# A list-scheduled fused kernel: durations of the schedule reset, last tokens of y written by ACT and DVE into a ring of 11 slots, weight sums and weight splits given places

## The chip, the cores and the metric

The kernel runs on one core of one Trainium2 chip. The metric is the device time of one execution in microseconds (us). Differences under about 0.5% (4.9 us here) can't be told from no change.

## What is computed

Three blocks follow each other, for 8 batches of 576 tokens and a model width of 512. All arithmetic is float32; the kernel splits each operand into a high and a low part (names ending in h and l) and adds three matrix products.

```python
# attention without a score matrix: softmax of q over features, of k over tokens
x = softmax(q) @ (softmax(k, axis=tokens).T @ v)
# gated block: w_in 512x1024, token mixing w_sg 576x576, w_out 512x512
u, v = split(gelu_tanh(x @ w_in), 2)
v_n = layernorm(v) * g_ln
x = x + (u * (w_sg @ v_n + b_sg)) @ w_out
# gated convolution: w_in2 512x1024, 3 taps along tokens, w_out2 1024x512
h = relu(x @ w_in2)
y = h * sigmoid(conv3(h, conv_w))
out = y @ w_out2
```

## The kernel before

**Two stages.** The first stage (about 0 to 570 us of the span) does attention and the gated block for batches 0 to 7 and writes x to DRAM. Its loop `for b in range(B)` calls 29 groups per batch (hv, hu, pair, mx and wo in the program), and `insert` puts pieces of the attention of later batches between them. The second stage, the convolution block (from about 570 us), works feature block by feature block: 8 blocks `fc` of 128 features per batch. For one block, TensorE (PE) makes `h` (from x and w_in2, 4 steps of 128 features, for two halves of the tokens), ACT applies relu, DVE and ACT convolve into `cv`, ACT takes the sigmoid, DVE multiplies with h, and `gate` (L1219) splits y = `cv` into `yh` (ACT) and `yl` (DVE). PE then multiplies yh and yl with w_out2 (`o2`, L1247), four token tiles of 128 into the four banks `acc`. The 64 tokens that are left of 576 are collected for two batches in `yLh` and `yLl`, which have 8 blocks of 128 columns, one half for each batch, and `o2_pair` (L1261) multiplies them once per pair of batches.

**Batches 0 and 1** of the second stage run straight (`h2`, L1202). Batches 2 to 7 use a scheme with 7 products in place of 8 (`quad`, L1404), which needs sums of w_in2's quarters (`weight_sums`, L1310: 11 additions on POOL for each of two halves c, tiles `tk`, results `tn0` to `tn2`) and sums of quarters of x (`operands`, L1340). x arrives as two DRAM tensors: `load_x` loads the high part into `xf`, `add_low` (L1295) loads the low part into an `xg` tile of 3 buffers and lets POOL add it.

**POOL's copies.** `gate` lets POOL copy the last 64 columns of each yh and yl into yLh and yLl (L1228). A list `later` holds copies back while `o2` of an earlier odd batch is open, since yLh has one set of slots.

**Weight splits.** w_in2 and w_out2 are cut into 32 jobs of 256 columns (`split_far`, L1043; `split`, L460). A job has a load, 3 ACT, 4 DVE and 3 POOL operations on tiles `wsl` and `farh`, and two stores. All 32 jobs are entered at the start of batch 1 of the first stage.

**What sets the order.** No engine runs in the order in which the code is written. The code records nodes in a `Plan`; `price` (L205) gives each node a cost and a latency, `deadlines` (L243) counts back from the PE's sequence the time `late` by which each must be issued, and `order` (L259) simulates the engines and lets each take the ready node with the least `late`. The order that comes out is fixed before the run; on the chip every engine issues its list in order and waits at its head. All recorded instructions have the line of `emit`, L403, in the profile, so they are told apart by tile names.

Of the kernel before, what the change touches and what calls it, by code (L numbers as in the profile page):

```python
# [25 lines left out]
CFG = {'dord': 'qqkqqkqwkkwwv', 'start': 'kaaatabbktbkbqkTawtqbqtQvwwvxxqxswxlwLc', 'gh': 'aaa', 'x2': 'nnn', 'hvl': [6, 5, 3], 'qs': 'ppppd', 'qm': 'pppdp', 'vb': 2, 'gb': 2, 'kt': 'dddd', 'sgl': 'dppp', 'rh': 'pd', 'sw': 'ada', 'sl': 'ada', 'gl': 'ddd'}  # L26
GUARD = 1.125 * 2.0 ** -15
# [105 lines left out]
class Node:  # L133
    __slots__ = ("eng", "name", "args", "kw", "cost", "lat", "deps", "succ", "late", "unit", "shared", "table", "kb", "i", "left", "ready", "done", "t", "hook")
# [10 lines left out]
class Plan:  # L145
# [59 lines left out]
    def price(self, n, out, ins):  # L205
# [18 lines left out]
        elif e == "act":  # L224
            n.cost = 0.15 + cols * 0.00091
            n.lat = n.cost + 0.12
            f = args_func(n)
            n.table = {"Gelu_apprx_tanh": "g", "Exp": "e", "Sigmoid": "s"}.get(f)
        elif e == "pool":
            if "tensor" in name:  # L230
                n.cost = 0.8 if cols == 1 else 0.2 + cols * (0.0008 if name == "tensor_copy" else 0.00195)
            else:
                n.cost = 0.05 + cols * 0.0009
            n.lat = n.cost + 0.1
            n.shared = True
        else:
            two = sum(v.tile.space != "psum" for v in ins) > 1 and not psum and name in ("tensor_tensor", "scalar_tensor_tensor")
            fast = not psum and name in ("tensor_scalar", "tensor_copy") and out.tile.dtype == F32
            n.cost = 0.07 + cols * (0.0066 if name == "reciprocal" else 0.00058 if fast else 0.00117)
            n.lat = n.cost + 0.07  # L240
            n.shared = (two or fast) and cols > 60

    def deadlines(self):  # L243
# [14 lines left out]

    def order(self):  # L259
# [152 lines left out]
def attn_gated_conv_kernel(ctx, tc, q, k, v, q0, k0, w_in, g_ln, w_sgT, b_sg, w_out, w_in2, conv_w, w_out2, out):  # L412
# [630 lines left out]
    def split_far(src, d, k, n, behind):  # L1043
        for c in range(k):
            for f in range(0, n, NW):
                fs = slice(f, f + NW)
                slot, h = parts[njob[0] % 2]
                njob[0] += 1
                split(slot, src[:, c, fs], far_h, slot[1].bitcast(F32R), NW, (pool, pool), [t[:, c, fs] for t in d], behind)
# [98 lines left out]
    for b in range(B):  # L1148
# [13 lines left out]
        for i, g in enumerate(groups):  # L1162
# [17 lines left out]
    yL = [p2.tile([128, NFC, 128], F32R, name=f"yL{n}") for n in "hl"]  # L1180
    later = []
# [37 lines left out]
    def gate(b, fc, h, cv):  # L1219
        yh = p2.tile([128, S], F32R, tag="yh", bufs=4)  # L1220
        yl = p2.tile([128, S], F32R, tag="yl", bufs=4)
# [4 lines left out]
        o = 64 * (b % 2)  # L1226
        yL_hi, yL_lo = yL
        def copies():  # L1228
            pool.tensor_copy(yL_hi[:, fc, o:o + 64], r32(yh[:, 512:576]))
            pool.tensor_copy(yL_lo[:, fc, o:o + 64], r32(yl[:, 512:576]))  # L1230

        if any(o_[0] < b and b % 2 == 0 for o_ in oq):
            later.append(copies)
        else:
            copies()
# [25 lines left out]
    def o2_pair(b, fcs):  # L1261
# [4 lines left out]
        for fc in fcs:  # L1266
            mm3(lp["t"], yL_hi[:, fc], yL_lo[:, fc], wo2_hi[:, fc], wo2_lo[:, fc], fc == 0, fc == NFC - 1)
# [27 lines left out]
    def add_low(b, xf, c):  # L1295
        xg = p2.tile([128, S], F32, tag="xg", bufs=3)
# [134 lines left out]
    for b in range(FIRST):  # L1431
        for fc in range(NFC):
# [96 lines left out]
```

## Time and profile before

| what | value |
|---|---|
| time, median of 3 runs (lowest, highest) | 981.03 us (979.24, 983.11) |
| the profiled execution: time, span in the profile | 981.86 us, 980.1 us |
| PE busy | 934.7 us (95%) in 6026 matmul records |
| DVE busy | 784.5 us (80%) |
| ACT busy | 556.9 us (57%) |
| POOL busy | 458.2 us (47%) |
| mean granted TensorE clock | 0.988 |
| chain that ended last, by engine | PE 60%, DVE 11%, POOL 3%, issue 3%, ACT 2%, DMA 1% |

The span reaches from the first to the last instruction; 1.8 us of the execution lie around it. An engine's share of busy time is an average over stages with different limits, so the stretches of 20 us matter more than the shares. The granted clock is given as a share of 2.4 GHz.

### The profile page before, as it was taken

The page shows a single profiled execution, that of the slowest core. Times are in us where ns is not written, and L with a number is a line of the kernel's source. Part 1 is how long each engine was busy: PE and PEld are TensorE (multiplying, and loading weights), DVE is VectorE, ACT ScalarE, POOL GpSimd, SP SyncE. Part 2 cuts the span into 40 slices and gives each one's busy share as a digit, 9 for nine tenths or more (in the row PEclk, how much of TensorE's full clock was granted, in tenths as well). Part 3 has the DMA queues.
Part 4 walks back from the last instruction along what each step waited for, and adds up shares of the span by engine and source line. Part 5 has one row for each costly group of instructions (what it writes and reads, how often), then busy time and mean ns, then how long its engine had stood idle before and what let it go on. Part 6 is the DMA issues. An engine that isn't in the chain of part 4 may idle for free.

```text
span 980.1 us, 16191 instructions
## 1 busy us (share of the span) xinstructions
PE 934.7 (95%) x6026; PEld 825.9 (84%) x6026; DVE 784.5 (80%) x1391; ACT 556.9 (57%) x1063; POOL 458.2 (47%) x500
## 2 busy tenths in 40 slices
PE   5989989998999999999999998999999999999996
PEld 4567778987989889899999997888998889888985
DVE  6988989799788897976867379997888878887773
ACT  6878356845666458453634244444766566656662
POOL 5326363556353754554434079644354626362110
PEclk9999989999999999999999999999999999999999
DMA  9451534250352625534256631313121313121001
GB/s 294 139 171 66 148 121 133 104 170 17 127 175 91 178 65 167 148 108 141 85 191 202 226 133 45 107 35 106 46 96 45 106 46 105 36 82 33 18 27 54
DMA packets 55590, 107.42 MB, mean 110 GB/s; under 512 B 5716, under 2 KB 29268, under 8 KB 52824
## 3 DMA queue, kind: packets, MB, share of 16 engines
q1 hardware_dynamic: 55512, 106.39, 34.5%
q8 instruction: 47, 0.77, 0.3%
q14 instruction: 31, 0.25, 0.1%
HBM read 70.85 MB, written 35.53 MB: 109 GB/s over the span
## 4 chain that ended last, share of the span: by engine, by line
PE 60%; DVE 11%; POOL 3%; issue 3%; ACT 2%; DMA 1%; SPq 0%; DVEq 0%; ACTq 0%; POOLq 0%
PE mm L403 39%; PE acc L403 21%; DVE cv L403 4%; POOL tk L403 1%; DVE yl L403 1%; POOL xf L403 1%; DMA out<-ot 1%; DVE xl L403 1%; DVE wsl L403 1%; DVE scr L403 1%; DVE lt L403 0%; DVE h L403 0%; DVE gl L403 0%; ACT cv L403 0%; DVE ot L403 0%
## 5 line engine op out<-in xcount | busy, mean ns | idle before, releaser
L403 DVE SCALAR_TENSOR_TENSOR cv<-h,cw,cv 128x576 f32<-128x576 f32 x128 | 132.3, 1034 | 27.8 <-ACT cv L403 25.7
L403 POOL CAST yLh<-yh 128x64 fp32r<-128x64 f32 x64 | 38.6, 603 | 152.6 <-ACT yh L403 152.6
L403 PE MATMUL acc<-wAh,yl 128*128 128x512 f32 x256 | 102.8, 402 | 6.6 <-DVE yl L403 6.6
L403 PE MATMUL acc<-wAh,yh 128*128 128x512 f32 x256 | 102.8, 402 | 0.3 <-ACT yh L403 0.2
L403 PE MATMUL acc<-wAl,yh 128*128 128x512 f32 x256 | 102.3, 400 | 0.0
L403 PE MATMUL acc<-gl,wouth 128*128 128x288 f32 x256 | 78.5, 307 | 4.8 <-DVE gl L403 4.8
L403 PE MATMUL mm<-xh,w2h 128*128 128x288 f32 x280 | 82.6, 295 | 0.4 <-ACT ot L403 0.4
L403 PE MATMUL acc<-gh,wouth 128*128 128x288 f32 x256 | 82.9, 324 | 0.0
L403 PE MATMUL mm<-xl,w2h 128*128 128x288 f32 x280 | 82.5, 295 | 0.0
L403 PE MATMUL mm<-xh,w2l 128*128 128x288 f32 x280 | 82.3, 294 | 0.0
L403 PE MATMUL mm<-sgh,vnh 128*128 128x288 f32 x256 | 80.8, 315 | 0.0
L403 PE MATMUL mm<-xh,wAh 128*128 128x288 f32 x256 | 80.5, 315 | 0.1
L403 POOL TENSOR_TENSOR wsl<-wsl 128x256 f32<-128x256 f32 (+2 forms) x66 | 50.1, 761 | 59.8 <-ACT wsl L403 18.6
L403 PE MATMUL acc<-gh,woutl 128*128 128x288 f32 x256 | 77.9, 304 | 0.0
L403 PE MATMUL mm<-xh,wAl 128*128 128x288 f32 x256 | 75.7, 296 | 1.4 <-ACT wAl L403 1.4
L403 PE MATMUL mm<-sgh,vnl 128*128 128x288 f32 x256 | 75.5, 295 | 0.0
L403 PE MATMUL mm<-sgl,vnh 128*128 128x288 f32 x256 | 75.5, 295 | 0.0
L403 PE MATMUL mm<-xl,wAh 128*128 128x288 f32 x256 | 75.5, 295 | 0.0
L403 ACT ACTIVATE cv<-cv 128x576 f32<-128x576 f32 x64 | 43.7, 683 | 54.9 <-DVE cv L403 54.6
L403 POOL TENSOR_TENSOR q<-q,qm 128x512 f32<-128x512 f32 x56 | 61.6, 1129 | 20.5 <-DVE qm L403 13.4
L403 DVE TENSOR_TENSOR cv<-cv,h 128x576 f32<-128x576 f32 x64 | 59.2, 926 | 14.3 <-ACT cv L403 13.5
L403 PEld LDWEIGHTS acc<-wAh,yl 128*128 128x128 f32 x256 | 48.9, 191 | 20.7 <-DVE yl L403 8.8
(276 smaller groups left out, 3028.9 us busy)
## 6 DMA issues: line engine op xcount, KB each, us to landing
vt<-in_v SPq DMA_DIRECT2D x8, 1152.0 KB, 10.2
x2d<-x2s SPq DMA_DIRECT2D x16, 576.0 KB, 3.8
out<-ot SPq DMA_DIRECT2D x32, 256.0 KB, 2.0
kt<-in_k SPq DMA_DIRECT2D x7, 1152.0 KB, 5.7
xld<-xl SPq DMA_DIRECT2D x7, 1152.0 KB, 5.3
xf<-x2d SPq DMA_DIRECT2D x7, 1152.0 KB, 5.1
xg<-xld SPq DMA_DIRECT2D x28, 288.0 KB, 2.8
q<-in_q SPq DMA_DIRECT2D x28, 256.0 KB, 2.7
```

Source lines behind the costliest of these rows:

```text
L403: getattr(self.real[n.eng], n.name)(*[val(a) for a in n.args], **{k: val(v) for k, v in n.kw.items()})
```

## The change

**Durations.** The costs in `price` are set anew: ACT, POOL, DVE. For DVE the fixed part goes from 0.07 to 0.15 us and the slope falls from 0.00117 to 0.00104 us per column; a POOL operation on one column goes from 0.8 to 0.95 us. In `order`, POOL's lengthening while DVE is on its second read port is now up to 0.5 us instead of 30% of the overlap.

**Last tokens.** POOL's 128 copies and the list `later` go. `gate` writes yh and yl with 512 columns; the last 64 tokens are written by a second ACT and a second DVE instruction into yLh and yLl at once. These have 11 slots in place of 8, in a ring (`last_slot`), so that a new pair of batches can begin before `o2_pair` of the pair before has run. `xg` has 2 buffers in place of 3.

**Places.** The splits are entered one by one from group 37 (batch 1, group 8) to group 177, each with a due time 90 us after PE's last node then (`soon`, `FAR`), and each load not before that node starts. `weight_sums` is entered at (batch 0, block 6) and (1, 2) in place of (1, 0) and (1, 2), and its first additions may not start before PE's last node then.

```diff
+FAR = 90.0
+FIRST = 2
+SUMS = ((0, 6), (1, 2))
+YB = 4
...
         elif e == "act":
-            n.cost = 0.15 + cols * 0.00091
-            n.lat = n.cost + 0.12
+            n.cost = (0.155 if psum else 0.195) + cols * 0.00085
+            if isinstance(n.kw.get("scale"), View) or isinstance(n.kw.get("bias"), View):
+                n.cost += 0.05 + min(cols, 500) * 0.0001
+            n.lat = n.cost + 0.07
...
-                n.cost = 0.8 if cols == 1 else 0.2 + cols * (0.0008 if name == "tensor_copy" else 0.00195)
+                wide = any(o[0] == "to_broadcast" for v in views for o in v.ops)
+                n.cost = 0.95 if cols == 1 else 0.2 + cols * (0.0008 if name == "tensor_copy" else 0.00164 if wide else 0.0021)
...
-            n.cost = 0.07 + cols * (0.0066 if name == "reciprocal" else 0.00058 if fast else 0.00117)
+            n.cost = 0.15 + cols * (0.0062 if name == "reciprocal" else 0.00055 if fast else 0.00104)
+            if len(ins) > 2 or (fast and len(ins) > 1):
+                n.cost += min(cols, 500) * 0.00013
...
+            if n.due:
+                n.late = n.due[0].late + n.due[1]
...
-                    more = min(cost, vecend[0] - t) * 0.3
+                    more = min(0.5, vecend[0] - t)
...
-            if b == 1 and i == 0:
-                mark = next(n for n in reversed(plan.nodes) if n.eng == "pe")
-                split_far(w_in2_v, w2d, KC, FF2, mark)
-                split_far(w_out2_v, wo2d, NFC, DM, mark)
+            if far and 29 * b + i >= 37 + 140 * (32 - len(far)) / 32:
+                plan.soon(FAR, split_far)
...
+    def last_slot(b, fc):
+        turn_ = fc if b < FIRST else 2 * (fc % 4) + (fc < 4)
+        return (b // 2 * NFC + turn_) % NL
...
-        act.activation(yh, cv, AF.Copy)
-        dve.tensor_tensor(yl, cv, r32(yh), ALU.subtract)
...
+        act.activation(yh, cv[:, 0:512], AF.Copy)
+        dve.tensor_tensor(yl, cv[:, 0:512], r32(yh), ALU.subtract)
+        sl = last_slot(b, fc)
...
+        act.activation(zh, cv[:, 512:S], AF.Copy)
+        dve.tensor_tensor(zl, cv[:, 512:S], r32(zh), ALU.subtract)
...
-        xg = p2.tile([128, S], F32, tag="xg", bufs=3)
+        xg = p2.tile([128, S], F32, tag="xg", bufs=2)
...
+        after = plan.last
...
-            pool.tensor_tensor(t, r32(wq[n][0][:, c]), r32(wq[n][1][:, c]), ALU.add)
+            pool.tensor_tensor(t, r32(wq[n][0][:, c]), r32(wq[n][1][:, c]), ALU.add).deps[after.i] = "start"
...
-            if b == 1 and fc in (0, 2):
-                weight_sums(fc // 2)
+            if (b, fc) in SUMS:
+                weight_sums(SUMS.index((b, fc)))
```

Since every engine's list comes from `order`, all lists are written anew. PE keeps its 5608 matmuls, DVE has 64 TENSOR_TENSOR more, ACT 64 ACTIVATE more, POOL 128 CAST fewer, and ACT's list has 31 ACT_TABLE_LOAD in place of 45. In the lists below the line of `emit` is L403 before and L421 in the change.

**Place 1, DVE in the first stage, near 126 us of the span.** `u` and `gl` belong to the gated block (gl is what PE's `acc` matmuls need), `lm`, `lx` and `qm` to the maxima and sums of the attention's softmax. Before:

```order
L403 TENSOR_TENSOR u_722<-mm_153,u_722 128x288
L403 COPY lx_802<-lm_712 32x8 x3
L403 SCALAR_TENSOR_TENSOR lm_712<-lm_712,lx_802 128x8
L403 RECIPROCAL lm_712<-lm_712 128x8
L403 TENSOR_REDUCE qm_664<-q_0_239 128x16
L403 TENSOR_TENSOR gl_779<-u_722,gh_775 128x288
L403 TENSOR_TENSOR u_674<-mm_186,u_674 128x288
```

In the change:

```order
L421 COPY lx_784<-lm_780 32x8 x2
L421 TENSOR_TENSOR lm_780<-lm_780,lx_784 128x8
L421 TENSOR_TENSOR u_674<-mm_146,u_674 128x288
L421 TENSOR_TENSOR u_688<-mm_181,u_688 128x288
L421 TENSOR_REDUCE qm_782<-q_0_212 128x16
L421 TENSOR_TENSOR gl_721<-u_674,gh_716 128x288
L421 TENSOR_TENSOR gl_775<-u_688,gh_752 128x288
```

Between a `u` and its `gl` stood six small or medium instructions; now stand two.

**Place 2, POOL at the start of the second stage.** `tk` are the weight sums, `xf<-xf,xg` the additions of x's low part, CAST the copies of the last tokens. Before:

```order
L403 TENSOR_TENSOR tk_5662<-w2h_4965,w2l_4994 128x512
L403 TENSOR_TENSOR tk_5682<-w2h_4965,w2l_4994 128x512
L403 TENSOR_TENSOR tk_5662<-tk_5682,tk_5662 128x512
L403 TENSOR_TENSOR tk_5706<-w2h_4965,w2l_4994 128x512
L403 TENSOR_TENSOR tk_5725<-tk_5706,tk_5682 128x512
L403 TENSOR_TENSOR tk_5706<-tk_5706,tk_5662 128x512
L403 TENSOR_TENSOR tn0l_5754<-tk_5662,tn0h_5708 128x512
L403 TENSOR_TENSOR tk_5766<-w2h_4965,w2l_4994 128x512
L403 TENSOR_TENSOR tk_5662<-w2h_4965,w2l_4994 128x512
L403 TENSOR_TENSOR tk_5766<-tk_5662,tk_5766 128x512
L403 CAST yLh_5814<-yh_5793 128x64
```

In the change:

```order
L421 TENSOR_TENSOR xf_5669<-xf_5669,xg_5675 128x576
L421 TENSOR_TENSOR xf_5669<-xf_5669,xg_5681 128x576
L421 TENSOR_TENSOR xf_5669<-xf_5669,xg_5675 128x576
L421 TENSOR_TENSOR xf_5669<-xf_5669,xg_5681 128x576
L421 TENSOR_TENSOR tk_5974<-w2h_4974,w2l_5037 128x512
L421 TENSOR_TENSOR tk_5991<-w2h_4974,w2l_5037 128x512
L421 TENSOR_TENSOR tk_5974<-tk_5991,tk_5974 128x512
L421 TENSOR_TENSOR tk_6017<-w2h_4974,w2l_5037 128x512
L421 TENSOR_TENSOR tk_6031<-tk_6017,tk_5991 128x512
```

Ten weight sums stood ahead of the first copy; now the four additions to x come first, and the sums begin only when PE has reached block 6 of batch 0.

**Place 3, DVE at the start of the second stage.** Before:

```order
L403 TENSOR_TENSOR cv_5701<-cv_5701,h_0_4961 128x576
L403 SCALAR_TENSOR_TENSOR cv_5746<-h_0_4967,cw_939,cv_5746 128x576
L403 TENSOR_TENSOR yl_5804<-cv_5701,yh_5793 128x576
L403 TENSOR_TENSOR cv_5746<-cv_5746,h_0_4967 128x576
L403 TENSOR_SCALAR cv_5701<-h_0_5660,cw_939 128x576
```

In the change:

```order
L421 TENSOR_TENSOR yl_5762<-cv_5697,yh_5746 128x512
L421 SCALAR_TENSOR_TENSOR cv_5744<-h_0_4981,cw_841,cv_5744 128x576
L421 TENSOR_TENSOR yLl_5777<-cv_5697,yLh_5754 128x64
L421 TENSOR_SCALAR cv_5697<-h_0_5661,cw_841 128x576
L421 SCALAR_TENSOR_TENSOR cv_5697<-h_0_5661,cw_841,cv_5697 128x576
```

`yl` is 64 columns shorter, and `yLl` comes after it as an instruction of its own, one place later.

## Rows read from the trace of the kernel before

**Rows 1.** Stretches: from:to and length in us, busy time and count of each engine.

```profile
core 0: us, PE busy (x) PEld busy (x) DVE busy (x) ACT busy (x) POOL busy (x), PEclk, DMA share, GB/s
100.00:140.00 40.00, 35.05 (x218) 31.29 (x218) 35.42 (x78) 15.27 (x24) 23.19 (x25) 0.87 0.50 147
220.00:240.00 20.00, 17.07 (x104) 15.48 (x103) 19.49 (x36) 10.60 (x24) 12.71 (x11) 0.91 0.07 21
540.00:560.00 20.00, 20.00 (x152) 20.00 (x152) 6.67 (x15) 4.78 (x11) 0.00 (x0) 1.00 0.61 211
580.00:640.00 60.00, 53.94 (x306) 46.84 (x305) 57.94 (x53) 27.47 (x51) 47.81 (x41) 0.97 0.22 71
573.00:680.00 107.00, 100.94 (x599) 90.02 (x598) 96.35 (x100) 50.68 (x95) 69.58 (x64) 0.98 0.24 77
720.00:740.00 20.00, 17.86 (x108) 16.08 (x107) 17.53 (x21) 11.69 (x23) 15.45 (x13) 1.00 0.28 90
820.00:840.00 20.00, 18.22 (x104) 16.21 (x103) 18.39 (x21) 12.80 (x26) 15.40 (x13) 0.92 0.33 103
```

**Rows 2.** PE's waits over the whole span: us in total, times, longest us.

```profile
PE acc L403 <- DVE yl L403: 6.6, 5, 2.5
PE acc L403 <- DVE gl L403: 4.8, 4, 2.7
...
PE mm L403 <- DVE u L403: 3.6, 2, 2.9
PE mm L403 <- DVE kvd L403: 3.2, 2, 2.2
```

**Rows 3.** DVE, then PE in order of time near place 1: start us, us.

```profile
126.49 2.68 DVE L403 COPY lx<-lm 32x8 f32<-32x8 f32 x3
...
130.55 0.45 DVE L403 TENSOR_TENSOR gl<-u,gh 128x288 fp32r<-128x288 f32 x1
...
131.05 0.61 PE L403 MATMUL acc<-gl,wouth 128*128 128x288 f32 x1 [2.72 <-DVE gl L403]
```

**Rows 4.** POOL in order of time at the start of the second stage.

```profile
565.22 2.53 POOL L403 TENSOR_TENSOR tk<-w2h,w2l 128x512 f32<-128x512 f32 x2 [34.00 <-PE mm L403]
...
570.54 2.67 POOL L403 TENSOR_TENSOR tk<-tk,tk 128x512 f32<-128x512 f32 x2
...
582.42 0.82 POOL L403 CAST yLh<-yh 128x64 fp32r<-128x64 f32 x1 [2.07 <-ACT yh L403]
```

**Rows 5.** DVE, then POOL in order of time between 735 and 738 us.

```profile
735.57 1.97 DVE L403 TENSOR_TENSOR yl<-cv,yh 128x576 fp32r<-128x576 f32 x1
737.46 0.81 DVE L403 SCALAR_TENSOR_TENSOR cv<-h,cw,cv 128x576 f32<-128x576 f32 x1
...
735.11 1.81 POOL L403 TENSOR_TENSOR xf<-xg,xf 128x576 f32<-128x576 f32 x1
736.88 0.76 POOL L403 CAST yLh<-yh 128x64 fp32r<-128x64 f32 x1
```

**Rows 6.** Instructions that write cv and yLh: ns min/median/max, first and last start.

```profile
L403 DVE SCALAR_TENSOR_TENSOR cv<-h,cw,cv x128: 801/819/2061, 574.1 to 960.2; 128x576 f32<-128x576 f32 x128
...
L403 DVE TENSOR_TENSOR cv<-cv,h x64: 742/759/1986, 580.9 to 961.7; 128x576 f32<-128x576 f32 x64
...
L403 POOL CAST yLh<-yh x64: 237/712/1108, 582.4 to 963.3; 128x64 fp32r<-128x64 f32 x64
```

**Rows 7.** Groups by shape: busy us, mean ns, idle before and its releasers.

```profile
L403 POOL TENSOR_TENSOR tk<-w2h,w2l 128x512 f32<-128x512 f32 x8 | 11.5, 1449 | 34.0 <-PE mm L403 34.0
...
L403 DVE SCALAR_TENSOR_TENSOR qm<-qm,qx 128x64 f32<-128x64 f32 x7 | 1.9, 270 | 1.2 <-ACT qx L403 1.1
...
L403 ACT ACT_TABLE_LOAD x45 | 57.7, 1283 | 3.1 <-PE mm L403 1.7 <-PEq L1519 0.7
...
L403 ACT ACTIVATE qx<-qm 32x64 f32<-32x64 f32 x48 | 12.2, 255 | 6.0 <-DVE qm L403 5.2
```

**Rows 8.** The weight splits' tile wsl alone, columns as in group 1.

```profile
80.00:560.00 480.00, 0.00 (x0) 0.00 (x0) 63.80 (x128) 39.46 (x96) 72.20 (x96) 0.99 0.42 130
```

More of the change, by code (lines that the diff above doesn't have):

```diff
@@ L133 @@
 class Node:
-    __slots__ = ("eng", "name", "args", "kw", "cost", "lat", "deps", "succ", "late", "unit", "shared", "table", "kb", "i", "left", "ready", "done", "t", "hook")
+    __slots__ = ("eng", "name", "args", "kw", "cost", "lat", "deps", "succ", "late", "unit", "shared", "table", "kb", "i", "left", "ready", "done", "t", "hook", "due")
 class Engine:
@@ L149, in __init__, with soon @@
     def __init__(self, real):
-        self.real, self.nodes, self.unit = real, [], 0
+        self.real, self.nodes, self.unit, self.due, self.last = real, [], 0, None, None
         for k in real:
             setattr(self, k, Engine(self, k))
+    def soon(self, lead, job):
+        self.due = (self.last, lead)
+        job()
+        self.due = None
     def begin(self):
@@ L159, in node @@
         n.eng, n.name, n.args, n.kw, n.i, n.unit = eng, name, args, kw, len(self.nodes), self.unit
-        n.deps, n.succ, n.table, n.kb, n.shared, n.cost, n.lat, n.hook = {}, [], None, 0, False, 0.0, 0.0, None
+        n.deps, n.succ, n.table, n.kb, n.shared, n.cost, n.lat, n.hook, n.due = {}, [], None, 0, False, 0.0, 0.0, None, self.due
         self.nodes.append(n)
+        if eng == "pe":
+            self.last = n
         return n
@@ L1041, in attn_gated_conv_kernel, with split_far @@
     njob = [0]
[L1043 to L1049, printed above, removed]
+    far = []
+    for src, d, kc, n in ((w_in2_v, w2d, KC, FF2), (w_out2_v, wo2d, NFC, DM)):
+        far += [(src, d, c, slice(f, f + NW)) for c in range(kc) for f in range(0, n, NW)]
+    def split_far():
+        src, d, c, fs = far.pop(0)
+        slot, h = parts[njob[0] % 2]
+        njob[0] += 1
+        split(slot, src[:, c, fs], far_h, slot[1].bitcast(F32R), NW, (pool, pool), [t[:, c, fs] for t in d], plan.last)
     far_h = p1.tile([128, NW], F32R, name="farh")
@@ L1179, in attn_gated_conv_kernel @@
     wo2_hi, wo2_lo = w2["ohi"], w2["olo"]
-    yL = [p2.tile([128, NFC, 128], F32R, name=f"yL{n}") for n in "hl"]
-    later = []
+    NL = NFC + 3
+    yL = [p2.tile([128, NL, 128], F32R, name=f"yL{n}") for n in "hl"]
+    held = {}
+    def last_slot(b, fc):
+        turn_ = fc if b < FIRST else 2 * (fc % 4) + (fc < 4)
+        return (b // 2 * NFC + turn_) % NL
     h_t = [w2["pool"].tile([128, S + 2], F32, name=f"h{i}") for i in range(3)]
@@ L1219, in gate @@
     def gate(b, fc, h, cv):
-        yh = p2.tile([128, S], F32R, tag="yh", bufs=4)
-        yl = p2.tile([128, S], F32R, tag="yl", bufs=4)
+        yh = p2.tile([128, 512], F32R, tag="yh", bufs=YB)
+        yl = p2.tile([128, 512], F32R, tag="yl", bufs=YB)
         act.activation(cv, cv, AF.Sigmoid)
         dve.tensor_tensor(cv, cv, h[:, 1:S + 1], ALU.mult)
-        act.activation(yh, cv, AF.Copy)
-        dve.tensor_tensor(yl, cv, r32(yh), ALU.subtract)
[L1226 to L1235, printed above, removed]
+        act.activation(yh, cv[:, 0:512], AF.Copy)
+        dve.tensor_tensor(yl, cv[:, 0:512], r32(yh), ALU.subtract)
+        sl = last_slot(b, fc)
+        assert held.get(sl, (b // 2, fc)) == (b // 2, fc)
+        held[sl] = (b // 2, fc)
+        zh, zl = (t[:, sl, 64 * (b % 2):64 * (b % 2) + 64] for t in yL)
+        act.activation(zh, cv[:, 512:S], AF.Copy)
+        dve.tensor_tensor(zl, cv[:, 512:S], r32(zh), ALU.subtract)
         y_t[b, fc] = (yh, yl)
@@ L1266, in o2_pair @@
         for fc in fcs:
-            mm3(lp["t"], yL_hi[:, fc], yL_lo[:, fc], wo2_hi[:, fc], wo2_lo[:, fc], fc == 0, fc == NFC - 1)
+            sl = last_slot(b, fc)
+            held.pop(sl)
+            mm3(lp["t"], yL_hi[:, sl], yL_lo[:, sl], wo2_hi[:, fc], wo2_lo[:, fc], fc == 0, fc == NFC - 1)
         if NFC - 1 in fcs:
@@ L1283, in do_o @@
             o2_pair(b_, range(NFC))
-            while later:
-                later.pop(0)()
-    FIRST = 2
     xg2 = {}
@@ L1341, in operands @@
         q = {"11": xf[:, 0:2, 0:HALF], "12": xf[:, 2:4, 0:HALF], "21": xf[:, 0:2, HALF:S], "22": xf[:, 2:4, HALF:S]}
-        s1 = p2.tile([128, S], F32, tag="xg", bufs=3).rearrange("p (c t) -> p c t", c=2)
+        s1 = p2.tile([128, S], F32, tag="xg", bufs=2).rearrange("p (c t) -> p c t", c=2)
         mine = opn[b] = {}
```

## The prediction

> **What bounds the kernel now.** I read the page first, then the stretches of 20 us, then PE's waits, then the lists in order of time around the largest waits. The chain that ended last is PE for 60% of the span and PE is busy for 95% of it, so time can only be won where PE waits or runs at the lower clock. The stretches show where that is [rows 1]. Between 100 and 140 us PE is idle for 40 - 35.05 = 4.95 us, and the granted clock of 0.87 says that 0.13 x 40 = 5.2 us more went to matmuls at 1.2 in place of 2.4 GHz: 10.1 us. Between 220 and 240 us it is 2.9 + 0.09 x 20 = 4.7 us. At the start of the second stage, 580 to 640 us, it is 6.1 + 0.03 x 60 = 7.9 us. At two turns from one batch to the next, 720 to 740 and 820 to 840 us, it is 2.1 and 1.8 + 1.6 us: 5.5 us. The other stretches from 640 us on hold almost nothing until the last 20 us. These places hold 10.1 + 4.7 + 7.9 + 5.5 = 28.2 us, and they are all that the change can reach. The first 100 us have waits too, but there loads and the first splits set the pace, and PE's list begins with the same 104 rows.
>
> In all these places PE waits for DVE [rows 2]: for `yl` 6.6 us in 5 waits, for `gl` 4.8 in 4, for `u` 3.6 in 2, for `kvd` 3.2 in 2. DVE is late for two reasons. In the first stage it does things in a poor order: a `gl` that PE needs at once stands behind three copies of 32x8 that together took 2.68 us, and PE waits 2.72 us [rows 3]. In the second stage POOL holds it up: while POOL adds two tiles, a DVE instruction with two inputs takes about twice as long. A `yl` beside a POOL addition took 1.97 us [rows 5], where a product of the same size takes 0.742 at best and 0.759 in the median [rows 6].
>
> **The change, part by part.** The sum is made against the profiled execution, 981.86 us; the median is 0.8 us lower.
>
> *Matmuls.* None is added or removed, so PE's own work stays.
>
> *POOL's copies.* 128 copies go, of 0.71 us in the median for the 64 of yLh [rows 6]. They cost DVE nothing: a DVE instruction beside copies alone took 0.81 us [rows 5], the median of its kind is 0.819 [rows 6]. POOL has room (47% busy), so its own time is not on the path either. What they do cost is place in POOL's list: POOL stood 2.07 us before the first copy, waiting for yh [rows 4], with additions to x queued behind. I give this 0 by itself and count it in the terms for the second stage.
>
> The Trainium skill speaks otherwise (SBUF — State Buffer, section "Who interferes with whom"): VectorE with two SBUF inputs and a GpSimd instruction that reads SBUF exclude each other for a whole instruction, and that would hold for a copy too. The rows above do not bear it out for these copies; by the page the copies would have cost DVE their own length, and the result is my first rival.
>
> *The second instructions for the last tokens.* 64 on ACT and 64 on DVE. No row shows this form. On DVE the nearest, of 128x64, took 0.27 us [rows 7]; yl becomes shorter by 64 of 576 columns, 0.08 of 0.76 us. So each block costs DVE 0.19 us; the ends are 0 and 0.27. ACT: 0.255 us for 32x64 [rows 7], less 0.07. ACT is busy for 27.5 of 60 us in the worst stretch [rows 1], so its 64 x 0.18 = 12 us lie beside PE. DVE's 12 us lie beside PE too, except at 573 to 680 us: 16 blocks x 0.19 = 3 us there. The ring of 11 slots lets the first 3 blocks of a new pair be written before `o2_pair`; from the fourth on, ACT's instruction waits for a matmul that stands ahead anyway, and behind it ACT's next sigmoid. I price that at 0; it is seen as ACT waiting for PE before yLh.
>
> *Weight sums.* Of 22 additions, six were issued between 565.2 and 573 us, before DVE had any block (the first two and the last two of them are shown [rows 4]); 540 to 560 us shows DVE at 6.7 of 20 us and POOL at 0 [rows 1]. The change starts them only at block 6 of batch 0 (place 2). So six more additions of 1.45 us [rows 7] fall beside DVE's blocks, at about 1 us of DVE each (1.97 - 0.76 = 1.2 in the worst case): 6 us. Against that, the additions to x come first, and the first blocks meet a quiet POOL. Between 573 and 680 us DVE is busy for 96.4 of 107 us [rows 1]; with 6 + 3 us it has 105 us to do in a stretch that would be 107 - 8 = 99 us if PE never waited. So DVE still binds there on average, and only the lag it may carry into 680 us and later, two to three blocks by the rings of 4 `yl` and 5 `h`, lets PE win. I take 3 of the 7.9 us: **-3 us** (ends -8 and +9).
>
> *Turns between batches.* At 720 and 820 us POOL runs its additions for x in one block while a copy waits in their midst. In the change nothing stands in their midst, while two in place of three `xg` buffers space them by loads. I take half of 5.5 us: **-3 us** (ends -5.5 and +2).
>
> *Durations and splits in the first stage.* The old prices gave DVE 0.07 to 0.15 us for an instruction of 8 to 64 columns; 0.27 us and, for the three copies, 0.9 us each were measured [rows 3, 7]. The new ones give 0.15 to 0.22. Place 1 shows the effect: two in place of six instructions between `u` and `gl`. ACT's list has 14 table loads less, 14 x 1.283 = 18 us [rows 7], spread over a stage in which ACT is mostly waiting. Of the 14.8 us lost at 100 to 140 and 220 to 240 us I take a third: **-5 us**. The ends are -14.8, and +6, because a newly drawn list of some 1,300 DVE instructions opens waits elsewhere. A split takes 63.8/32 = 2.0 us of DVE and 72.2/32 = 2.3 us of POOL [rows 8]. In POOL's list, 20 in place of 15 of the 32 now stand ahead of batch 7's attention, so 5 x 2.0 = 10 us of DVE work come earlier, into stretches with DVE at about 17 of 20 us. That is inside the +6.
>
> Sum: -3 - 3 - 5 = **-11 us**: 981.9 - 11 = 970.9, or **970 us** against the median.
>
> **Rivals.**
>
> *The copies do cost DVE their length* (faster still). Against it stand the rows on 0.81 and 0.819 us. For it: copies and additions often follow each other, so a mixed case may hide a cost. The shortest time of such a copy, 0.237 us [rows 6], times 128 is 30 us of DVE; then 573 to 680 us is no longer bound, all of 7.9 + 5.5 us goes, and with 5 us from the first stage it is 981 - 18 = **963 us**. This is the outcome by the page named above. Chance 0.15.
>
> *The gains are given back* (no change). New lists close known waits and open others of the same size, in a first stage where DVE is at 17 to 19 of 20 us; the splits that come earlier meet it there. For it: DVE's load hardly changes, only its order. The first stage at 0, the second at -2: **979 us**. Chance 0.21.
>
> *The sums crowd the second stage* (slower). Place: 600 to 660 us. Held back to block 6 of batch 0, 22 additions of up to 1.8 us beside DVE and some ten additions for x make POOL full for 50 us, and every one stretches a DVE instruction by about 1 us. If the lag exceeds what the rings hold, PE pays the whole 9 us of extra DVE work on top of what it pays now, and the first stage gives nothing: 981 + 9 - 2 = **988 us**. It decides where DVE is over 19.5 of 20 us for more than two stretches running. For it: DVE is at 57.9 of 60 us now [rows 1]. Against: the lists' planner knows of this stretching and writes PE's list accordingly. Chance 0.14.
>
> **The numbers.** Forecast 0.50, with its own range of 963 to 976; rivals 0.15, 0.21 and 0.14. Under 0.5% (4.9 us) a measurement can't tell a change, so faster means under 976.1: 0.50 + 0.15 = 0.65; same 0.21; slower 0.14. The range of 958 to 984 leaves out the slow rival and the tail of the fast one.
>
> **What would show it.** Right: PE's waits for `gl`, `u` and `kvd` fall by half from 11.6 us; waits for `yl` stay above 2 us; DVE beside POOL's sums still takes 1.5 to 2 us; DVE stays over 19 of 20 us in some stretch between 600 and 660 us; `yLl` takes 0.2 to 0.3 us. Wrong: the waits for `yl` vanish (first rival), or grow past 12 us (third), or the first stage ends no earlier than now (second).

## The result and the profile after

The changed kernel takes 969.85 us in the median of 4 runs (969.03 to 972.05), the kernel before 981.26 us (979.24 to 983.11). The ratio is 0.9888, with a 95% interval of 0.9861 to 0.9914. The profiled execution took 969.03 us, its span 967.3 us. The total came out as forecast; where it came from did not.

**How the span divides.** The first matmul on w2h opens the second stage. The instructions that write or read w2h, of the kernel before and then of the change, have its time as the first start (columns: ns min/median/max, first and last start, forms):

```profile
L403 PE MATMUL mm<-xh,w2h x280: 289/294/402, 569.7 to 953.2; 128*128 128x288 f32 x140
```

```profile
L421 PE MATMUL mm<-xh,w2h x280: 289/294/402, 557.2 to 940.6; 128*128 128x288 f32 x140
```

The first stage is 569.7 - 557.2 = 12.5 us shorter. The second went from 980.1 - 569.7 = 410.4 us to 967.3 - 557.2 = 410.1 us: nothing. These two lengths are the yardstick for every run below.

**The first stage.** Stretches of 100 us (columns as in [rows 1]), before, then after:

```profile
100.00:200.00 100.00, 94.42 (x684) 84.46 (x684) 85.27 (x194) 59.91 (x107) 51.33 (x55) 0.95 0.42 125
200.00:300.00 100.00, 96.09 (x681) 86.41 (x678) 87.77 (x186) 56.21 (x109) 50.84 (x54) 0.98 0.40 121
300.00:400.00 100.00, 98.07 (x764) 89.92 (x763) 85.97 (x186) 62.65 (x126) 55.33 (x61) 1.00 0.42 133
```

```profile
100.00:200.00 100.00, 95.00 (x773) 85.12 (x772) 92.66 (x209) 53.41 (x106) 53.99 (x56) 1.00 0.43 133
200.00:300.00 100.00, 99.40 (x682) 89.36 (x682) 87.05 (x182) 51.84 (x107) 48.62 (x53) 1.00 0.44 127
300.00:400.00 100.00, 99.58 (x753) 90.52 (x752) 91.41 (x192) 64.01 (x129) 56.82 (x66) 1.00 0.53 161
```

The first number after the length is PE's busy time, the share behind the counts the granted clock. Before, PE was idle for 5.6 + 3.9 + 1.9 = 11.4 us and the clock cost 5 + 2 = 7 us. After, it is idle for 5.0 + 0.6 + 0.4 = 6.0 us and the clock is 1.00. That makes 12.4 us, which is the whole gain of the stage. More than half is the clock: before, it was lower in the stretches in which PE waited, between 100 and 240 us [rows 1]; after, PE waits less there and in this execution the clock doesn't fall. Five kernels of the experiments whose PE is as busy from 100 to 200 us (94.5 to 95.0 us in a_nudge, a_tokens, a_sums, a_zlpool and a_xg2) were granted 0.98 there, so some 0.02 x 100 = 2 of the 12.4 us belong to this execution and not to the change.

**The second stage.** The stretches that answer to [rows 1]:

```profile
573.00:680.00 107.00, 97.96 (x559) 85.44 (x558) 95.35 (x113) 47.55 (x104) 52.21 (x32) 0.98 0.16 54
580.00:640.00 60.00, 53.96 (x314) 47.36 (x313) 54.14 (x60) 24.82 (x56) 31.11 (x20) 0.97 0.16 53
220.00:240.00 20.00, 19.40 (x133) 17.72 (x132) 18.23 (x35) 11.43 (x18) 11.54 (x11) 1.00 0.20 57
100.00:140.00 40.00, 36.53 (x336) 32.17 (x335) 37.85 (x92) 20.05 (x37) 21.60 (x23) 1.00 0.43 134
540.00:560.00 20.00, 20.00 (x152) 19.91 (x152) 7.21 (x21) 3.33 (x8) 0.00 (x0) 1.00 0.46 151
720.00:740.00 20.00, 19.92 (x116) 17.61 (x115) 18.69 (x23) 12.96 (x28) 11.71 (x7) 1.00 0.29 97
820.00:840.00 20.00, 20.00 (x117) 17.86 (x117) 18.80 (x32) 15.45 (x32) 3.67 (x3) 1.00 0.19 68
```

From 580 to 640 us, which now lie 12.5 us further into the stage, PE loses what it lost before, 6 us and 0.03 of clock, though POOL is now busy for 31 in place of 48 us there. The turns at 720 and 820 us are closed. PE's waits over the span, and the groups by shape that the change added or shrank, behind yl of the kernel before (columns as in [rows 2] and [rows 7]):

```profile
PE acc L421 <- DVE yl L421: 5.5, 4, 2.0
PE acc L421 <- ACT yh L421: 3.1, 3, 2.1
PE mm L421 <- DVE u L421: 2.8, 2, 2.0
...
PE acc L421 <- DVE gl L421: 1.0, 2, 0.6
...
PE mm L421 <- DVE kvd L421: 0.3, 1, 0.3
```

```profile
L403 DVE TENSOR_TENSOR yl<-cv,yh 128x576 fp32r<-128x576 f32 x64 | 57.3, 896 | 8.0 <-ACT yh L403 6.8 <-PE mm L403 0.8
```

```profile
L421 DVE TENSOR_TENSOR yl<-cv,yh 128x512 fp32r<-128x512 f32 x64 | 53.9, 843 | 14.1 <-ACT yh L421 14.1
...
L421 ACT ACT_TABLE_LOAD x31 | 39.8, 1283 | 1.4 <-PEq L1539 0.7 <-DVE vnl L421 0.2
...
L421 DVE TENSOR_TENSOR yLl<-cv,yLh 128x64 fp32r<-128x64 f32 x64 | 27.4, 428 | 0.3 <-ACT yLh L421 0.3
```

The last row is the surprise: an instruction of 64 columns takes 428 ns in the mean, half of what one of 512 takes. The mean hides two kinds (ns min/median/max, first and last start):

```profile
L421 DVE TENSOR_TENSOR yLl<-cv,yLh x64: 206/218/1470, 570.3 to 950.1; 128x64 fp32r<-128x64 f32 x64
```

52 of the 64 took 0.206 to 0.225 us; the 12 that started while POOL was adding took 0.695 to 1.470. DVE, then POOL, in order of time at the start of the second stage show it:

```profile
576.63 1.75 DVE L421 TENSOR_TENSOR yl<-cv,yh 128x512 fp32r<-128x512 f32 x1
578.31 1.30 DVE L421 TENSOR_TENSOR yLl<-cv,yLh 128x64 fp32r<-128x64 f32 x1
579.65 1.45 DVE L421 TENSOR_SCALAR cv<-h,cw 128x576 f32<-128x576 f32 x1
...
583.58 0.69 DVE L421 TENSOR_TENSOR yl<-cv,yh 128x512 fp32r<-128x512 f32 x1
...
584.92 0.22 DVE L421 TENSOR_TENSOR yLl<-cv,yLh 128x64 fp32r<-128x64 f32 x1
```

```profile
577.92 1.62 POOL L421 TENSOR_TENSOR tk<-tk,tk 128x512 f32<-128x512 f32 x1
579.49 1.29 POOL L421 TENSOR_TENSOR tk<-w2h,w2l 128x512 f32<-128x512 f32 x1
580.86 1.40 POOL L421 TENSOR_TENSOR tk<-tk,tk 128x512 f32<-128x512 f32 x1
```

POOL's last addition here ends at 582.26. Behind it yLl takes 0.22 us and yl 0.69; beside the additions they take 1.30 and 1.75. The 64-column instruction is stretched by 1.1 us, about as much as the 512-column one. DVE instructions that read TensorE's output (`acc` or `mm`) were not stretched in the second stage: `ot<-acc` took 0.68 us and `h<-mm,tk` 0.45 us (medians), beside POOL's additions as away from them.

### The profile page after: what moved, and what is told of

The parts are those of the page before. It is cut to its first block, busy times and chain, and to the rows that moved or that the text cites. A ratio compares the mean times of both kernels' runs of the same rounds, so it can differ in the third digit from the quotient of the medians.

```text
span 967.3 us, 16152 instructions
## 1 busy us (share of the span) xinstructions
PE 926.2 (96%) x6026; PEld 818.7 (85%) x6026; DVE 799.8 (83%) x1455; ACT 543.2 (56%) x1113; POOL 388.6 (40%) x372
## 4 chain that ended last, share of the span: by engine, by line
PE 77%; DVE 14%; ACT 4%; issue 2%; DMA 1%; POOL 1%; SPq 0%; ACTq 0%; DVEq 0%; POOLq 0%
PE mm L421 52%; PE acc L421 25%; DVE cv L421 4%; DVE yl L421 1%; DVE wsl L421 1%; DVE xl L421 1%; ACT L421 1%; DVE scr L421 1%; DVE gl L421 1%; DVE lm L421 0%; DMA sgh<-in_q 0%; DVE sm L421 0%; DVE q L421 0%; DVE r L421 0%; DVE lx L421 0%
## 5 line engine op out<-in xcount | busy, mean ns | idle before, releaser
L421 DVE SCALAR_TENSOR_TENSOR cv<-h,cw,cv 128x576 f32<-128x576 f32 x128 | 130.6, 1022 | 13.5 <-ACT cv L421 11.8
L421 POOL TENSOR_TENSOR xf<-xf,xg 128x576 f32<-128x576 f32 x28 | 47.1, 1696 | 158.9 <-DMA xf<-x2d 61.5
L421 PE MATMUL acc<-wAh,yl 128*128 128x512 f32 x256 | 102.5, 401 | 5.6 <-DVE yl L421 5.5
L421 PE MATMUL acc<-wAh,yh 128*128 128x512 f32 x256 | 102.2, 399 | 3.6 <-ACT yh L421 3.1
L421 PE MATMUL acc<-wAl,yh 128*128 128x512 f32 x256 | 101.4, 396 | 0.0
L421 PE MATMUL mm<-xh,w2h 128*128 128x288 f32 x280 | 82.5, 295 | 1.3 <-DVE h L421 1.3
L421 PE MATMUL mm<-xl,w2h 128*128 128x288 f32 x280 | 82.4, 294 | 0.0
L421 PE MATMUL mm<-xh,w2l 128*128 128x288 f32 x280 | 82.3, 294 | 0.0
L421 PE MATMUL mm<-xh,wAh 128*128 128x288 f32 x256 | 80.3, 314 | 1.5 <-ACT v L421 0.8
L421 PE MATMUL mm<-sgh,vnh 128*128 128x288 f32 x256 | 80.9, 316 | 0.8 <-DVE u L421 0.8
L421 PE MATMUL acc<-gh,wouth 128*128 128x288 f32 x256 | 80.4, 314 | 0.0
L421 POOL TENSOR_TENSOR wsl<-wsl 128x256 f32<-128x256 f32 (+1 forms) x66 | 51.0, 772 | 71.6 <-DVE wsl L421 36.1
L421 PE MATMUL acc<-gl,wouth 128*128 128x288 f32 x256 | 76.0, 297 | 1.0 <-DVE gl L421 1.0
L421 PE MATMUL acc<-gh,woutl 128*128 128x288 f32 x256 | 75.8, 296 | 0.0
L421 PE MATMUL mm<-xh,wAl 128*128 128x288 f32 x256 | 75.5, 295 | 0.0
L421 PE MATMUL mm<-xl,wAh 128*128 128x288 f32 x256 | 75.5, 295 | 0.0
L421 PE MATMUL mm<-sgl,vnh 128*128 128x288 f32 x256 | 75.3, 294 | 0.0
L421 PE MATMUL mm<-sgh,vnl 128*128 128x288 f32 x256 | 75.3, 294 | 0.0
L421 DVE TENSOR_TENSOR cv<-cv,h 128x576 f32<-128x576 f32 x64 | 58.9, 920 | 12.5 <-ACT cv L421 12.1
L421 POOL TENSOR_TENSOR q<-q,qm 128x512 f32<-128x512 f32 x56 | 61.2, 1118 | 19.4 <-DVE qm L421 19.4
L421 ACT ACTIVATE cv<-cv 128x576 f32<-128x576 f32 x64 | 43.6, 682 | 41.7 <-DVE cv L421 41.5
L421 POOL TENSOR_TENSOR kt<-kt,scr 128x512 f32<-128x512 f32 (+1 forms) x42 | 48.5, 1183 | 44.4 <-PE mm L421 31.0
```

What stands on the lines that cost most here:

```text
L421: getattr(self.real[n.eng], n.name)(*[val(a) for a in n.args], **{k: val(v) for k, v in n.kw.items()})
```

## The experiments

Each row below is one kernel: its median, its ratio to the kernel before timed on the same chip, and from its profile when the first matmul on w2h starts and how long the span lasts from there. Names with b_ are the kernel before with one part of the change done; names with a_ are the changed kernel with one part undone or altered. The lengths of the stages come from one execution each, and executions of one kernel differ: the 20 of the kernel before that were timed with the b_ kernels lie between 978.91 and 988.22 us. The profiled executions of b_splits and b_sums took 3.3 and 2.3 us more than their medians, so for differences of 2 to 3 us the ratio decides.

| kernel | part | us, median | ratio to before (95%) | first stage ends | second stage |
|---|---|---|---|---|---|
| before | | 981.26 | 1 | 569.7 | 410.4 |
| after | | 969.85 | 0.9888 (0.9861 to 0.9914) | 557.2 | 410.1 |
| b_dur | durations done | 987.62 | 1.0060 (1.0038 to 1.0081) | 558.1 | 429.5 |
| b_splits | splits done | 985.42 | 1.0046 (1.0029 to 1.0062) | 574.8 | 412.1 |
| b_tokens | last tokens done | 989.34 | 1.0079 (1.0055 to 1.0104) | 567.6 | 418.9 |
| b_sums | sums done | 982.58 | 0.9997 (0.9975 to 1.0018) | 568.6 | 414.5 |
| a_dur | durations undone | 996.68 | 1.0146 (1.0125 to 1.0168) | 575.8 | 421.1 |
| a_splits | splits undone | 987.21 | 1.0055 (1.0037 to 1.0074) | 554.9 | 430.4 |
| a_tokens | last tokens undone | 962.64 | 0.9801 (0.9779 to 0.9823) | 558.7 | 402.6 |
| a_sums | sums undone | 975.23 | 0.9932 (0.9914 to 0.9949) | 560.2 | 413.2 |
| a_zlpool | yLl on POOL | 960.63 | 0.9789 (0.9751 to 0.9827) | 558.5 | 401.6 |
| a_xg2 | a_tokens, two xg | 961.75 | 0.9805 (0.9771 to 0.9839) | 558.7 | 402.6 |
| a_copyact | a_tokens, copies on ACT | 960.46 | 0.9796 (0.9765 to 0.9826) | 557.1 | 401.4 |
| a_nudge | ACT 0.005 us longer in the schedule | 971.92 | 0.9910 (0.9878 to 0.9943) | 557.5 | 411.1 |

Some expectations speak of the stretch from the first matmul on w2h to the end of output projection 1. That end is the start of the last matmul on wA of batch 1: 680.5 us before and 674.0 after. What follows lasts 299.6 and 293.3 us. By these figures the start of the second stage lost 6.0 us and what follows gained 6.3. About half of that is work that changed places: 644 in place of 626 matmuls now run before that end. PE's idle time before it is 9.0 in place of 6.1 us; behind it, up to 958 us, it is 2.9 in place of 4.4 us, and 1.6 us lost to the clock are gone. So each side moved by some 3 us, and the table uses the whole stage.

### One part done on the kernel before

**b_dur.** `price` and the stretching of POOL alone:

```diff
-            n.cost = 0.15 + cols * 0.00091
+            n.cost = (0.155 if psum else 0.195) + cols * 0.00085
...
-            n.cost = 0.07 + cols * (0.0066 if name == "reciprocal" else 0.00058 if fast else 0.00117)
+            n.cost = 0.15 + cols * (0.0062 if name == "reciprocal" else 0.00055 if fast else 0.00104)
```

> The kernel before with the new durations of the schedule alone. Theory: the durations order the vector engines of the first stage better, and with the placed splits they make its 12.5 us; taken alone they give the larger part, so the first matmul of the second stage starts 6 to 10 us sooner than the 569.7 us of before, the 110.8 us from there to the end of output projection 1 stay within 2 us, the 299.6 us after that too: 972 to 975 us in all. Rival: the splits alone made the first stage, and the durations leave it within 2 us: 979 to 982 us.

The first stage ends 11.6 us sooner, a little more than the theory said, and the second is 19.1 us longer: 987.62 us, slower than before. Neither theory had that. PE's waits name it, and so does the last POOL operation on the splits' tile (POOL's row of that tile in this kernel, then in the changed one):

```profile
PE mm L408 <- ACT h L408: 12.1, 1, 12.1
```

```profile
L408 POOL TENSOR_TENSOR wsl<-wsl x66: 610/733/1447, 44.4 to 586.3; 128x256 f32<-128x256 f32 x32, 128x256 fp32r<-128x256 f32 x32, 128x512 f32<-128x512 f32 x2
```

```profile
L421 POOL TENSOR_TENSOR wsl<-wsl x66: 610/746/1449, 42.7 to 508.8; 128x256 f32<-128x256 f32 x32, 128x256 fp32r<-128x256 f32 x32, 128x512 f32<-128x512 f32 x2
```

With the new durations and no due time the weight splits end at 586.3 us, after the first stage; before they ended by some 530 us, and in the change they end by 510. What that does is shown at a_splits.

**b_splits.** The jobs entered one by one with due times, at the old durations:

```diff
-            if b == 1 and i == 0:
-                mark = next(n for n in reversed(plan.nodes) if n.eng == "pe")
-                split_far(w_in2_v, w2d, KC, FF2, mark)
-                split_far(w_out2_v, wo2d, NFC, DM, mark)
+            if far and 29 * b + i >= 37 + 140 * (32 - len(far)) / 32:
+                plan.soon(FAR, split_far)
```

> The kernel before with the 32 pairs of split jobs placed along the first stage with a due time, nothing else. Theory: alone they give 3 to 6 us of the first stage (the gl and u waits of TensorE shrink), nothing behind it: 975 to 978 us. Rival: they are all of the first stage's 12.5 us: 968 to 970 us. Second rival: without right durations the scheduler does nothing good with due times: 980 to 983 us.

All three miss, the second rival least. In the profiled execution, 3.3 us above the median, the first stage is 5.1 us longer and the second 1.7. From 200 to 400 us DVE is busy for 183.7 us here, for 173.7 before, and PE's waits for gl go from 4.8 to 5.5 us. That the early jobs meet a badly ordered DVE fits this, but isn't shown by itself.

**b_tokens.** The ring, ACT's and DVE's writing in place and two xg buffers, as in the diff of the change.

> The kernel before with the last 64 tokens of y written in place by ACT and DVE in the ring of 11 slots (and two xg buffers), nothing else. Theory: the turns between batches gain what they gained in the changed kernel, some 6 us of the 299.6 us behind output projection 1, while the first stage stays: 973 to 977 us. Rival: the second DVE instruction of each chunk, which waits for a POOL addition, costs 3 to 6 us in the 110.8 us before that, which would then be 114 to 117 us: 979 to 983 us.

At 989.34 us it is above both ranges. It costs 8.5 us of the second stage, both ways: 115.8 in place of 110.8 us at its start, where the rival had it, and 303.1 in place of 299.6 us behind it, where the theory had a gain. So the turns between batches didn't gain from the copies' going.

**b_sums.** The two places and the start condition alone:

```diff
+            pool.tensor_tensor(t, r32(wq[n][0][:, c]), r32(wq[n][1][:, c]), ALU.add).deps[after.i] = "start"
...
-            if b == 1 and fc in (0, 2):
+            if (b, fc) in SUMS:
```

> The kernel before with the weight sums in their new place alone (behind the matmuls of batch 0, chunk 6, and of batch 1, chunk 2, instead of wherever POOL is free at the stage's start). Theory: this is what lost 6 us at the start of the second stage: the 110.8 us from the first matmul there to the end of output projection 1 become 115 to 118 us, the rest stays: 985 to 988 us. Rival: the place costs nothing or gains, the stretch stays at 109 to 112 us: 979 to 982 us.

The time doesn't change, as the rival said. In the profile the second stage is 4.1 us longer and the first 1.1 shorter, but that execution took 2.3 us more than the median, so a loss in the second stage isn't shown.

### One part undone on the changed kernel

**a_dur** puts the old `price` back (b_dur's diff turned round).

> The changed kernel with the old durations of the schedule, all else new. Theory: the first matmul of the second stage moves back by 6 to 10 us from 557.2 us, what follows stays: 976 to 980 us. Rival: the splits made the first stage, the durations nothing: 968 to 971 us.

The durations are worth far more here: the first stage loses 18.6 us and the second 11.0. Splits with due times and a ring, scheduled with wrong durations, are 1.5% slower than the kernel before.

**a_splits** enters all jobs at the start of batch 1 again (b_splits' diff turned round).

> The changed kernel with the split jobs issued in one lump at the start of batch 1 again, all else new. Theory: the first stage loses 3 to 6 us: 973 to 976 us. Rival: it loses all of its 12.5 us: 980 to 983 us. Second rival: with the right durations the scheduler finds places for the jobs without due times: 969 to 971 us.

All three miss: the first stage is 2.3 us shorter, and the second loses 20.3 us. PE's wait, and ACT in order of time at its end:

```profile
PE mm L421 <- ACT h L421: 12.0, 1, 12.0
```

```profile
579.61 0.43 ACT L421 ACTIVATE wsl<-wsl 128x256 f32<-128x256 f32 x1 [1.23 <-DVE wsl L421]
580.58 0.42 ACT L421 ACTIVATE farh<-wsl 128x256 fp32r<-128x256 f32 x1 [0.54 <-DVE wsl L421]
580.90 1.30 ACT L421 ACTIVATE h<-mm 128x288 f32<-128x288 f32 x4
```

Four h, for which PE waits, stand in ACT's list behind the last step of the last split. Six jobs run between 557 and 583 us, one after the other, since two slots serve all 32 and each step waits for another engine or a DMA. The same wait, 12.1 us, is in b_dur. The wait is not the whole 20.3 us: over the second stage PE is idle for 33.2 in place of 19.3 us and busy for 397.2 in place of 390.8, at a granted clock of 0.97 in place of 0.99. So the durations move the jobs past the edge of the stage, where they hold up ACT, and the due times bring them back. Each of the two parts is harmful without the other.

**a_tokens** brings POOL's copies back, with three xg buffers (the last-token part of the diff turned round).

> The changed kernel with POOL's copies of the last tokens again (and three xg buffers), all else new. Theory: the stretches behind output projection 1 lose about 6 us (293.3 us become 298 to 300 us), the start of the second stage stays within 2 us of 116.8 us: 974 to 977 us. Rival: the start of the second stage gains 3 to 6 us, since no 64-column DVE instruction waits for a POOL addition: 969 to 973 us.

The rival was right, and by more than it said: 962.64 us, the second stage 7.5 us shorter than in the changed kernel, and nothing lost behind output projection 1 (292.8 against 293.3 us). The same stretch as above, 580 to 640 us, is now full:

```profile
580.00:640.00 60.00, 60.00 (x369) 54.75 (x368) 59.51 (x53) 25.48 (x50) 52.23 (x42) 1.00 0.17 58
```

**a_sums** puts the sums in their old place, without a start condition:

```diff
-SUMS = ((0, 6), (1, 2))
+SUMS = ((1, 0), (1, 2))
...
-            pool.tensor_tensor(t, r32(wq[n][0][:, c]), r32(wq[n][1][:, c]), ALU.add).deps[after.i] = "start"
+            pool.tensor_tensor(t, r32(wq[n][0][:, c]), r32(wq[n][1][:, c]), ALU.add)
```

> The changed kernel with the weight sums in their old place (as soon as POOL is free), all else new. Theory: the start of the second stage wins its 6 us back: the 116.8 us from its first matmul to the end of output projection 1 become 110 to 112 us: 963 to 966 us. Rival: the sums are not to blame, the stretch stays at 115 us or more: 968 to 972 us. Second rival: at their old place the sums hold up the additions for xf, and batch 1 starts later: 973 to 978 us.

It loses where the theory had a gain: 3.0 us in the first stage and 3.1 in the second. The second rival's number fits, its reason doesn't, since the first stage is hit as well. In the second stage PE's idle time hardly moves (19.7 against 19.3 us); PE is busy for 2.7 us longer, at a granted clock of 0.91 to 0.94 in each 20 us from 580 to 640 us, where the changed kernel has 1.00, 1.00 and 0.91. In the kernel before, the place was worth nothing (b_sums, 0.9997), so its worth depends on the rest of the lists; how was not settled.

### What the last tokens cost

Three theories of the 7.5 us were stated before the next four runs: the 64-column DVE instructions (D), the third xg buffer (X), and chance in the list schedule (N).

**a_zlpool** moves one instruction:

```diff
-        dve.tensor_tensor(zl, cv[:, 512:S], r32(zh), ALU.subtract)
+        pool.tensor_tensor(zl, cv[:, 512:S], r32(zh), ALU.subtract)
```

> The changed kernel with the 64-column subtraction of the last tokens on POOL instead of DVE; ring, two xg buffers and ACT's copy stay. After a_tokens gave 7.0 us in the start of the second stage (109.8 against 116.8 us), three theories of what the last tokens cost there. D: the 16 further DVE instructions, which take 0.22 us alone and 1.3 us beside a POOL addition, 8.3 us in the stretch: without them it becomes 109 to 112 us and the whole 962 to 966 us. X: two xg buffers instead of three hold up the loads for batch 2: the stretch stays at 115 to 118 us, 969 to 972 us in all. N: the list schedule comes out 5 us better or worse by chance with any edit: anything from 108 to 120 us.

D holds: the stretch is 109.1 us, with ring, two xg buffers and ACT's copy still there, and the whole, 960.63 us, is 1.4 us under D's range. The instruction on POOL, and PE's waits for yl and yh over the span:

```profile
L421 POOL TENSOR_TENSOR yLl<-cv,yLh x64: 322/682/925, 567.8 to 942.9; 128x64 fp32r<-128x64 f32 x64
```

```profile
PE acc L421 <- ACT yh L421: 2.6, 2, 1.9
PE acc L421 <- DVE yl L421: 2.5, 4, 0.9
```

**a_xg2** is a_tokens with two buffers:

```diff
-        xg = p2.tile([128, S], F32, tag="xg", bufs=3)
+        xg = p2.tile([128, S], F32, tag="xg", bufs=2)
...
-        s1 = p2.tile([128, S], F32, tag="xg", bufs=3).rearrange("p (c t) -> p c t", c=2)
+        s1 = p2.tile([128, S], F32, tag="xg", bufs=2).rearrange("p (c t) -> p c t", c=2)
```

> The kernel a_tokens (POOL's copies again) with two xg buffers as in the changed kernel. D: the stretch from the first matmul of the second stage to the end of output projection 1 stays at 109 to 112 us, 962 to 965 us in all. X: it goes back to 115 us or more, 968 us in all. N: it moves by up to 6 us either way.

The stretch is 112.1 us, just over D's bound and 3 under X's; the second stage as a whole is 402.6 us with either number of buffers, and the time 961.75 us. X falls.

**a_copyact** is a_tokens with the two copies on ACT:

```diff
-            pool.tensor_copy(yL_hi[:, fc, o:o + 64], r32(yh[:, 512:576]))
-            pool.tensor_copy(yL_lo[:, fc, o:o + 64], r32(yl[:, 512:576]))
+            act.activation(yL_hi[:, fc, o:o + 64], r32(yh[:, 512:576]), AF.Copy)
+            act.activation(yL_lo[:, fc, o:o + 64], r32(yl[:, 512:576]), AF.Copy)
```

> The kernel a_tokens with ACT making both copies of the last tokens instead of POOL; DVE keeps one 576-column subtraction for each chunk. D: DVE is as free of the 64-column instruction as in a_tokens, ACT takes some 0.25 us more for each copy and has room: the stretch becomes 108 to 112 us, 960 to 965 us in all. Rival: POOL's copies helped by themselves, by standing between its additions, and without them the stretch is 114 us or more: 967 to 971 us.

The stretch is 112.5 us, a little over the bound, the whole 960.46 us as D had it. POOL's copies don't help by themselves. Nor do they hurt: with 128 copies on POOL (a_xg2), 128 on ACT, or half on POOL as a subtraction, the second stage takes 402.6, 401.4 and 401.6 us.

**a_nudge** is the control for chance:

```diff
-            n.cost = (0.155 if psum else 0.195) + cols * 0.00085
+            n.cost = (0.16 if psum else 0.20) + cols * 0.00085
```

> The changed kernel with the schedule's duration of every ACT instruction 0.005 us longer, nothing else: a control for theory N. D and X: what the schedule does with nearly equal durations is nearly equal, every stage stays within 2 us: 968 to 972 us. N: the order of the second stage comes out otherwise and its start moves by 3 us or more: below 966 or above 974 us.

971.92 us, both stages within 1 us of the changed kernel in the profile, although DVE's and POOL's lists differ from early on. Its yLl rows are as bad as those of the change:

```profile
L421 DVE TENSOR_TENSOR yLl<-cv,yLh 128x64 fp32r<-128x64 f32 x64 | 28.0, 437 | 0.3 <-ACT yLh L421 0.3
```

One nudge is one draw, but it speaks against N, and so do four removals or additions of the DVE instruction (b_tokens, a_tokens, a_zlpool, a_copyact) that moved the second stage by 8.5, 7.5, 8.5 and 8.7 us, each in D's direction. a_zlpool and a_copyact beat both kernels: their intervals end at 0.9827 and 0.9826, that of the change begins at 0.9861.

## Why the prediction was right in the sum and wrong in its parts

- **Durations and splits in the first stage, -5 us: the mechanism right, the size wrong.** Measured -12.5, between the ends of -14.8 and +6. The loss that [rows 1] show there went for the most part, the part at the lower clock with it; a third of it was too little. The waits for gl, u and kvd fell from 11.6 to 1.0 + 2.8 + 0.3 = 4.1 us, more than by half.
- **Durations and splits as one term: incomplete.** The prediction priced the splits' earlier place as a risk inside the +6. The runs show it as a condition: without it the better durations cost the kernel before 6 us (b_dur), and taking it from the changed kernel costs 17 us (a_splits).
- **The second instructions for the last tokens, 0.19 us a block on DVE: wrong.** This is the step that failed. It took a mean of seven instructions [rows 7] for the price. The tile's own rows in the kernel before show what that mean hides (ns min/median/max, first and last start):

```profile
L403 DVE TENSOR_TENSOR qm<-qm,qx x7: 173/262/1200, 84.0 to 385.1; 128x64 f32<-128x64 f32 x7
L403 DVE SCALAR_TENSOR_TENSOR qm<-qm,qx x7: 186/226/580, 99.0 to 393.2; 128x64 f32<-128x64 f32 x7
```

  One of 64 columns had taken 1.2 us already, beside an addition on POOL, and the lists put the new ones into the very stretch where POOL adds. The 64 took 0.428 us in the mean, and yl became shorter by 0.053 (0.896 to 0.843): 0.375 a block, outside the ends of 0 and 0.27. The 16 up to the end of output projection 1 took 8.3 us, and their yl became shorter by some 0.9 us in all; the prediction had 3 us for the two. They cost 8.5 us alone (b_tokens) and 7.5 to 8.7 us in the changed kernel.
- **Start of the second stage and turns, -3 and -3: right only as a sum with other signs.** The stage gave 0.3. It would have given some 8 us (a_tokens, 402.6 against 410.4), and the last tokens took that back. The turns did gain, some 3 us of PE's lost time out of the 6.3 us of span, but by the durations: with them and POOL's copies the time behind output projection 1 is 293.7 us (b_dur), with the ring and the old durations 303.3 us (a_dur). So "nothing stands in their midst" was not the reason.
- **ACT's second instruction and the ring, 0: right.** ACT's yLh took 0.245 us, and ACT waited 0.8 us before all 64, none of it for PE. 31 table loads in place of 45 came as read from the list.
- **The copies, 0: right.** Three places for them give the same second stage within 1.2 us.
- **First rival, 963 us, copies that cost DVE their length: no.** But a kernel at 963 us or better was there, in the changed kernel without the 64-column instructions on DVE.
- **Second rival, gains given back: no for the total, yes for the second stage.** **Third rival, sums that crowd the stage: no.** Undoing their place lost 6.1 us of the span (a_sums).
- **The signs: four of five.** The waits for gl, u and kvd fell by more than half, those for yl stayed at 5.5 us, DVE beside POOL's sums took 1.75 us (yl above), and from 640 to 660 us DVE was busy for 19.8 of 20 us. `yLl` took 0.2 to 0.3 us only where POOL wasn't adding, in 52 of 64 cases.

The two errors, 7.5 us of gain too little in the first stage and nearly 6 us too much in the second, cancelled: that the total came out was luck. A forecast of the total alone would not have shown either.

The Trainium skill (SBUF — State Buffer, "Who interferes with whom") says of the port pair that VectorE and GpSimd share that it is held for a whole instruction and that the other one blocks. For POOL's additions the rows agree: yLl takes 1.30 us beside one and 0.22 us alone, and the one-input TENSOR_SCALAR behind it 1.45 us. For POOL's copies they differ, as far as DVE's time goes: in the kernel before, the 40 SCALAR_TENSOR_TENSOR on cv that ran beside copies alone took 0.813 us in the mean, the 53 beside no POOL instruction 0.817. It is the copies that were stretched (0.237 us at best, 0.712 in the median), and taking them from POOL moved the second stage by 1.2 us at most.

## What to carry to other kernels

Before moving small work to an engine that shares a resource, price the instruction by what it waits for and not by its columns: in this kernel a 64-column DVE instruction that started while POOL was adding took 0.5 to 1.25 us longer, and one of 512 columns at most 1.24 us longer. Put short pieces on an engine with room that doesn't meet that wait (here ACT), or keep them inside a wider instruction. In this list schedule, better durations and due times belonged together: a task that nothing soon needed was put off by the better durations until it stood in front of something urgent. And add up a forecast by stages, since two wrong terms can make a right sum.

## What the runs showed that was not expected

- A DVE subtraction of 64 columns took 0.206 to 0.225 us alone and up to 1.47 us in the same kernel. A subtraction of the same shape on POOL took 0.68 us in the median and cost the kernel nothing.
- The clock gave back more than the waits did in part of the first stage: from 100 to 200 us PE's idle time fell by only 0.6 us, while the granted clock went from 0.95 to 1.00, which is 5 us (3 us by the 0.98 of the five other profiles).
- Of the 24 us of further DVE time, 8.3 us of yLl lie before the end of output projection 1, the stretch in which a_tokens and a_zlpool gained 7.0 and 7.7 us; behind it the other 48 cost next to nothing (293.3 us, 292.8 in a_tokens). One way to the path is seen: ACT's next step on cv waited for yLl, 4.2 us in 6 times.
- Still open: the rest of that chain (DVE idles for longer over the span too, 14.1 us before yl in place of 8.0), and why the sums' new place helps the changed kernel and not the one before.
